# The first 32 places of experts 0 to 3 as a group of their own, ahead of the last choice

## The chip, the cores and the metric

The kernel runs on one core of a Trainium2 chip. The metric is the time of one execution on the device, in microseconds (us); the median of the runs counts.

## What is computed

The reference is a Fourier mixing layer followed by a mixture of experts with a capacity.

```python
X = np.fft.rfft(x, axis=1)                       # x: 8 x 2496 x 256
Yr = Xr @ w_r - Xi @ w_i + b_r                   # and Yi; then a soft threshold of 0.01 on both
y = np.fft.irfft(Yr + 1j * Yi, n=2496, axis=1)   # 19968 tokens of 256
expert_idx = np.argmax(y @ w_gate, axis=1)       # 8 experts
gate_w = softmax(y @ w_gate)[chosen expert]
for e in range(8):
    tok_idx = the 80 tokens of expert e with the largest gate_w
    h = np.maximum(y[tok_idx] @ w1[e], 0.0)      # w1: 256 x 1024
    out[tok_idx] = gate_w[tok_idx, None] * (h @ w2[e])   # w2: 1024 x 256
```

All other rows of the output are zero.

## The kernel before

The eight samples go one after another through stages of products (the transforms, the complex weights, the threshold), which `stageD` and others issue; that is some 490 us of the time. Per sample the gates of all tokens are computed, and the best candidates of every expert are kept. Of the mixed tokens only partial sums are stored to HBM, in two tensors `hd[0]` (7 rows of 256 f32 for each set of tokens) and `hd[1]` (6 rows): a token is a sum of these 13 rows with 13 weights out of the table `vt`.

**The choice.** The choice among the first samples is held as `bg`: a list `t0b` of 80 values for each of the 8 experts, sorted, and a list of their places (`t1b`, then `pfb`). The last samples give a list of 48 (`NEW`), and `merge` compares it from the end with the places 32 to 79 of the first list, and puts the better of the two there. The places 0 to 31 are those of the first samples whatever the last ones bring. A flag tells whether the two lists may have been too short, and then a slow branch at the end repeats the choice (here it isn't taken). `choose` spreads the 8 x 80 places over 640 partitions in 5 groups of 128: `flat` multiplies on VectorE (L1017) with an identity of 8, and TensorE sums over 8 partitions (L1021), and L1284 to L1286 make `posA`, the addresses. `rows` does the same for the gate values.

**The gathers.** For each of the 5 groups GpSimd issues, through `gather` (L1109), a gather of token numbers (`tok`), of 128 x 1792 values (`hx`, from `hd[0]`), of 13 weights (`wv`) and of 128 x 1536 values (`hx`, from `hd[1]`). `begin` writes them out for groups 0 to 2; those of groups 3 and 4 follow as buffers come free (3 buffers for the larger part, 2 for the smaller).

**The sums.** `position` makes the weighted sum of a group's 13 rows. For groups 0 and 1 some rows (`PEQ`) go to TensorE as products with a diagonal matrix of weights (`columnsY`, L1224, which also transposes), the others to ScalarE (L1162) and VectorE (L1170). For groups 2 to 4 ScalarE (L1185, L1190), VectorE (L1197, L1198) and GpSimd (L1193) share them, and TensorE transposes the sum (L1228). In both cases ScalarE writes the columns as f16 to `xT` (L1231) and VectorE the f16 rest (L1232): one eviction.

**The experts.** Expert e uses the columns 80e to 80e+79 of `xT`: `ffn1` (L1245, 96 products of 128x80, first layer, evicted by L1247 on ScalarE and L1249 on VectorE) and `ffn2` (L1261, 96 products, evicted into `oT` by L1262). Expert 3 ends with place 319 and needs groups 0 to 2, expert 4 also group 3. `give` transposes 128 rows of results (L1266), multiplies by the gate (L1268) and scatters them (L1269).

**The weights.** Each expert's weights are loaded as f32 in 4 pieces of 512 KB (L823), cast to f16 on ScalarE (L840, L843, L846; `prepW`) and the residue is taken on GpSimd (L858) or VectorE (L848). Those of experts 6 and 7 come last: two pieces of expert 6 are loaded from SyncE at 510.06 us, behind the last stores, and expert 7's go into buffers of the gathers once these are free. Fillers on TensorE (L1701, 6 of them, and `busy`, L1210, up to 36) stand before the first group's products.

**What sets the order.** Each engine executes its own list in order; the lists come from a scheduler that places an instruction where its inputs are ready by its own estimate, except where `tc.issue_after(i)` or `behind(event)` puts it after a named instruction.

## Time and profile before

| | us |
|---|---|
| median of 3 runs | 583.82 (583.77 to 584.67) |
| profiled execution, its time | 588.99 |
| profiled execution, its span | 587.2 |
| TensorE busy | 532.3 (91%) |
| VectorE busy | 388.1 (66%) |
| GpSimd busy | 376.7 (64%) |
| ScalarE busy | 324.6 (55%) |

A share of busy time is a mean over the whole span. The change concerns only the last 100 us or so, where the choice ends, the groups are gathered and the experts run; that stretch has to be read by its own rows, below. Times in the rows are counted from the start of the span.

### The profile page before, as it was taken

The page shows a single profiled execution, that of the slowest core. Times are in us where ns is not written, and L with a number is a line of the kernel's source. Part 1 is how long each engine was busy: PE and PEld are TensorE (multiplying, and loading weights), DVE is VectorE, ACT ScalarE, POOL GpSimd, SP SyncE. Part 2 cuts the span into 40 slices and gives each one's busy share as a digit, 9 for nine tenths or more (in the row PEclk, how much of TensorE's full clock was granted, in tenths as well). Part 3 has the DMA queues.
Part 4 walks back from the last instruction along what each step waited for, and adds up shares of the span by engine and source line. Part 5 has one row for each costly group of instructions (what it writes and reads, how often), then busy time and mean ns, then how long its engine had stood idle before and what let it go on. Part 6 is the DMA issues. An engine that isn't in the chain of part 4 may idle for free.

```text
span 587.2 us, 12890 instructions
## 1 busy us (share of the span) xinstructions
PE 532.3 (91%) x5037; PEld 387.2 (66%) x5037; DVE 388.1 (66%) x739; ACT 324.6 (55%) x466; POOL 376.7 (64%) x301
## 2 busy tenths in 40 slices
PE   7869999999999999999999999988899988885883
PEld 3356676668677866877687778756767865444883
DVE  4423555666767667667667876768999687844750
ACT  2324868575756756565667565555654447321671
POOL 4005887686857677786768775777961575765671
PEclk9969999999999999999999999998999868885998
DMA  7897898997989799978979787999936796677530
GB/s 220 256 244 210 308 216 275 265 283 217 282 267 312 193 259 269 278 217 238 280 250 258 235 255 181 304 263 270 230 114 193 185 316 202 176 251 259 189 96 23
DMA packets 97225, 137.02 MB, mean 233 GB/s; under 512 B 26601, under 2 KB 77809, under 8 KB 95403
## 3 DMA queue, kind: packets, MB, share of 16 engines
q1 hardware_dynamic: 91115, 118.10, 69.8%
q0 software_dynamic: 2624, 11.45, 5.8%
q10 hardware_dynamic: 3418, 6.58, 3.5%
q8 instruction: 41, 0.67, 0.5%
q14 instruction: 27, 0.21, 0.1%
HBM read 70.82 MB, written 65.29 MB: 232 GB/s over the span
## 4 chain that ended last, share of the span: by engine, by line
PE 43%; DVE 15%; DMA 13%; issue 10%; POOL 9%; ACT 6%; SPq 2%; POOLq 0%; ACTq 0%; DVEq 0%
PE ps L443 21%; PE ps L311 5%; DMA wt<-in_moe_w 4%; PE ps L609 4%; DMA xt<-in_x 2%; DVE R L472 2%; POOL R L475 2%; ACT tp L467 2%; PE ps L546 2%; DMA out<-zero 2%; PE ps L547 2%; PE ps L382 1%; PE ps L383 1%; PE ps L384 1%; PE pf L1245 1%
## 5 line engine op out<-in xcount | busy, mean ns | idle before, releaser
L443 PE MATMUL ps<-XT,WM 128*128 128x288 f16 (+4 forms) x1536 | 215.7, 297 | 7.5 <-DVE Gs L561 2.1
L443 PEld LDWEIGHTS <-WM 128*128 128x128 f16 x1536 | 148.7, 98 | 64.2 <-issue 7.5
L472 DVE SCALAR_TENSOR_TENSOR R<-ps,thr,tp 128x674 f32<-128x674 f32 (+1 forms) x56 | 48.6, 868 | 75.8 <-ACT tp L467 72.1
L490 POOL TENSOR_TENSOR YT<-R,YT 128x1408 f16<-128x1408 f32 (+1 forms) x28 | 73.4, 2623 | 32.0 <-ACT YT L489 30.2
L467 ACT ACTIVATE tp<-ps,thr 128x674 f32<-128x674 f32 (+1 forms) x56 | 43.5, 777 | 80.4 <-PE ps L443 80.4
L475 POOL TENSOR_TENSOR R<-R,sgs 128x576 f32<-128x576 f32 x28 | 36.5, 1302 | 75.0 <-DVE R L472 75.0
L297 POOL TENSOR_TENSOR xs<-xt,xs 117x1024 f16<-117x1024 f32 (+1 forms) x39 | 76.2, 1955 | 9.9 <-ACT xs L296 9.8
L382 PE MATMUL ps<-t2s,z 128*128 128x128 f16 x320 | 59.7, 225 | 10.3 <-DMA z<-zs 7.4
L388 DVE TENSOR_TENSOR XT<-ps,XT 128x640 f16<-128x640 f32 (+2 forms) x64 | 51.7, 815 | 18.4 <-ACT XT L387 17.7
L333 DVE TENSOR_TENSOR zs<-ps,zs 128x1024 f16<-128x1024 f32 (+1 forms) x45 | 51.1, 1136 | 18.1 <-ACT zs L332 17.7
L383 PE MATMUL ps<-t2s,z 128*128 128x128 f16 x320 | 59.7, 225 | 0.0
L384 PE MATMUL ps<-t2s,z 128*128 128x128 f16 x320 | 59.7, 225 | 0.0
L387 ACT ACTIVATE XT<-ps 128x640 f16<-128x640 f32 (+2 forms) x64 | 44.4, 700 | 25.6 <-PE ps L384 24.4
L311 PE MATMUL ps<-xs,t1s 117*128 117x512 f16 x213 | 52.6, 379 | 1.0 <-POOL xs L297 0.8
L609 PE MATMUL ps<-YO,vqs 128*128 128x512 f16 (+1 forms) x252 | 48.7, 334 | 1.1 <-DVE hs L616 1.1
L332 ACT ACTIVATE zs<-ps 128x1024 f16<-128x1024 f32 (+1 forms) x45 | 42.9, 954 | 12.0 <-PE ps L311 6.9
L558 DVE TENSOR_TENSOR YO<-ps,YO 128x768 f16<-128x768 f32 (+1 forms) x50 | 45.4, 907 | 6.2 <-ACT YO L557 6.2
L489 ACT ACTIVATE YT<-R 128x1408 f16<-128x1408 f32 (+1 forms) x28 | 35.5, 1267 | 21.3 <-POOL R L486 21.2
L546 PE MATMUL ps<-wgi,YT 128*128 128x144 f16 (+1 forms) x302 | 44.3, 232 | 2.8 <-DVE R L472 1.6
L547 PE MATMUL ps<-wgi,YT 128*128 128x136 f16 (+1 forms) x302 | 43.5, 228 | 0.0
L557 ACT ACTIVATE YO<-ps 128x768 f16<-128x768 f32 (+1 forms) x50 | 38.4, 774 | 3.1 <-PE ps L547 1.1
L609 PEld LDWEIGHTS <-vqs 128*128 128x128 f16 x252 | 24.6, 99 | 23.3 <-issue 2.9
(320 smaller groups left out, 990.5 us busy)
## 6 DMA issues: line engine op xcount, KB each, us to landing
out<-zero SPq DMA_DIRECT2D x48, 384.0 KB
hd<-hs SPq DMA_DIRECT2D x94, 192.0 KB
z<-zs SPq DMA_DIRECT2D x35, 512.0 KB
xt<-in_x SPq DMA_DIRECT2D x41, 312.0 KB
z<-z SPq DMA_DIRECT2D x14, 528.0 KB
z<-z SPq DMA_DIRECT2D x14, 432.0 KB
wt<-in_moe_w ACTq DMA_DIRECT2D x10, 512.0 KB
pair<-in_moe_w SPq DMA_DIRECT2D x10, 512.0 KB
```

Of the source, the lines that this page charges most:

```text
L297: nc.gpsimd.tensor_tensor(xs[:, 1, :ng], xt[:, j0:j0 + ng], xs[:, 0, :ng], op=ALU.subtract)
L311: nc.tensor.matmul(pt[:, 512 * j:512 * j + 512], t1s[:, t], xs[:, h, 2 * j:2 * j + 2], start=(i == 0), stop=(i == 2))
L382: nc.tensor.matmul(o, zz(0), t2s[:, cl, 0, :], start=True, stop=False)
L383: nc.tensor.matmul(o, zz(0), t2s[:, cl, 1, :], start=False, stop=False)
L384: nc.tensor.matmul(o, zz(1), t2s[:, cl, 0, :], start=False, stop=True)
L443: nc.tensor.matmul(pt[:, o:o + e - a], WM[:, dh, m, wh, 128 * eh:128 * eh + 128], XT[:, dh, xh, c, a:e], start=(i == 0), stop=(i == len(te ...
L467: acts.append(nc.scalar.activation(fv(t), pv, AF.Relu, bias=thr[:, eh, ri, 0:1]))
L472: nc.vector.scalar_tensor_tensor(fv(Rf), pv, thr[:, eh, ri, 1:2], fv(t), op0=ALU.add, op1=ALU.min)
L490: nc.gpsimd.tensor_tensor(yv(1), rv, yv(0), op=ALU.subtract)
L546: nc.tensor.matmul(pt[:, off:off + w], yt(0), wgi[:, eh, 0:w], start=True, stop=False)
L547: nc.tensor.matmul(pt[:, off:off + w - w % 128 // 2], yt(1), wgi[:, eh, 0:w - w % 128 // 2], start=False, stop=True)
L609: nc.tensor.matmul(o, tab[:, v], yo(h), start=(i == 0), stop=(i == 2))
```

## The change

The places 0 to 31 of experts 0 to 3 (128 places, since nothing that comes later can change them) become a group of their own, number 4 (`NL`). A new function `ahead_` works out their addresses as soon as the combination of the last samples' sums is done, and gathers their tokens, rows and weights, into memory (`pair6`) that expert 6's weights get later. `scaleA` multiplies the 13 rows by their weights on ScalarE, and `columnsA` adds and transposes them by 26 f32 products with the identity (52 records in a trace). The remaining 512 places are four groups: 48 of each of the experts 0 to 3, then 80 of each of the experts 4 to 7. Experts 0 to 3 need groups 0 and 1, expert 4 groups 1 and 2, experts 6 and 7 group 3.

With this go other changes: `BUSY` 32 to 12; the products of `flat` are cut by the parts of the list (192 and 320 columns, and 128); the columns of groups 0 and 1 are evicted in two pieces each, and the outputs of experts 0 to 3 also in two; the stores of the last stage are staged in one memory; the residues of expert 5's second layer go from GpSimd to VectorE; the casts of expert 6's weights, and their residues, go behind work of groups 2 and 3; two loads of expert 6's weights go behind the flag; expert 7's weights are loaded into the memory of expert 0's.

```diff
+SURE = CAP - NEW
+EARLY = ((0, 4, 0, SURE),)
+LATER_ = ((0, 4, SURE, CAP), (4, 8, 0, CAP))
...
-        hs = wkb.tile([128, 3, 256], F32, name="hs", bufs=3) if (ch, x) != (1, 2) else newYO(0).bitcast(F32).rearrange("p h j e -> p (h j e)")[:, :768].rearrange("p (c e) -> p c e", e=256)
+        if ch and x == 1:
+            hlast.append(newYO(0).bitcast(F32).rearrange("p h j e -> p (h j e)"))
+        hs = hlast[0][:, 768 * x:768 * x + 768].rearrange("p (c e) -> p c e", e=256) if ch else wkb.tile([128, 3, 256], F32, name="hs", bufs=3)
...
-    WV = [(6, 0, 0), (6, 0, 1)] + [(6, 1, 0), (6, 1, 1)] + [(7, 1, 1)]
+    WV = [(5, 1, 0), (5, 1, 1), (6, 0, 0), (6, 0, 1)] + [(6, 1, 0), (6, 1, 1)] + [(7, 1, 1)]
...
-                wt = p5.tile([128, 7 - i, 256], F32, name=f"hx{i}", bufs=3 - i).rearrange("p r e -> p (r e)")[:, :1024]
+                wt = slots["pair0"][:, 1024 * (2 * k + i):1024 * (2 * k + i) + 1024]
...
-                with behind(("A", "ra", 4)) if (e, k) == (7, 1) else tc.issue_after((hevs if e == 6 else dev)[-1].ins):
+                with behind(("A", "ra", k)) if e == 6 else tc.issue_after(dev[-1].ins):
...
-            nc.vector.tensor_tensor(px, v.unsqueeze(1).to_broadcast([8, 8, n]), i8.unsqueeze(2).to_broadcast([8, 8, n]), op=ALU.mult)
+            o = 0
+            for e0, e1, r0, r1 in parts:
+                k, w = e1 - e0, r1 - r0
+                nc.vector.tensor_tensor(px[:, o:o + k * w].rearrange("p (e r) -> p e r", e=k), v[:, r0:r1].unsqueeze(1).to_broadcast([8, k, w]), i8[:, e0:e1].unsqueeze(2).to_broadcast([8, k, w]), op=ALU.mult)
+                o += k * w
...
-    BUSY = (6, 32)
+    BUSY = (6, 12)
...
+        if e < 4:
+            nc.scalar.activation(oT[:, :, w * e:w * e + w], pv[:, :, SURE:], AF.Copy)
+            nc.scalar.activation(oT[:, :, 128 * NL + SURE * e:128 * NL + SURE * e + SURE], pv[:, :, :SURE], AF.Copy)
...
+    def ahead_():
+        p = spare()[:8]
+        pt = psum()
+        nc.vector.tensor_copy(pt[:8, 512:512 + SURE], bg[1][:, :SURE])
+        pr = flat(pt[:8, 512:512 + SURE], EARLY, F16, px=p.bitcast(F16))
+        nc.vector.tensor_tensor(posA[:, NL:], pr, cbs[:, 0, NL:], op=ALU.add)
+        hA = p7.tile([128, 4096], F32, name="pair6")
+        ct, get = gather_ids("A", posA, NG, cid[0:R1])
+        wv = hA[:, 3328:3344]
+        with tc.issue_after(sums[-1].ins):
+            get(NL)
+            gather(hA[:, :1792], hd[0][:5 * 192], ct[:, NL, 1:2])
+            gather(wv, vt, ct[:, NL, 2:3])
+            egs.append(gather(hA[:, 1792:3328], hd[1][:5 * 192], ct[:, NL, 1:2]))
+        return ct, [hA[:, 256 * r:256 * r + 256] for r in range(13)], wv
+
+    def scaleA(hx, wv):
+        for r in range(13):
+            nc.scalar.activation(hx[r], hx[r], AF.Copy, scale=wv[:, r:r + 1])
+
+    def columnsA(nm, hx):
+        pt = pct.tile([128, 512], F32, name="pt", bufs=1)
+        for h in range(2):
+            for r in range(13):
+                warms.append(nc.tensor.matmul(pt[:, 128 * h:128 * h + 128], hx[r][:, 128 * h:128 * h + 128], ident, start=(r == 0), stop=(r == 12)))
+        pv = pt[:, 0:256].rearrange("p (h e r) -> p h e r", h=2, e=4)
+        xv = lambda l: xT[:, l].rearrange("p h (e r) -> p h e r", e=E)[:, :, 0:4, :SURE]
+        ev[nm, "ya"] = nc.scalar.activation(xv(0), pv, AF.Copy)
+        nc.vector.tensor_tensor(xv(1), pv, xv(0), op=ALU.subtract)
...
-        got.append(gather_h(nm, 2, ct, True, lambda: get(4)))
+        got.append(gather_h(nm, 2, ct, True))
...
     combine(YO)
+    stacks[5].close()
+    p7 = ctx.enter_context(tc.tile_pool(name="p7", bufs=1, side="right", reuse_waits="tile"))
+    ctA, hxA, wvA = ahead_()
...
-        sA = begin("A", NG, posA, cid[0:R2])
+        with tc.issue_after(fls[-1].ins):
+            columnsA("A", hxA)
+        with tc.issue_after(warms[-1].ins):
+            busy(BUSY[1], pairs[0, 0][0])
+        sA = begin("A", NL, posA, cid[0:R2], ctA)
```

How this moves instructions is shown at three places.

GpSimd, from the combination's last addition to the first late gathers (`L858` before and `L867` now are residues of weights, `pair_6558` is the early group's memory), before:

```order
L574 TENSOR_TENSOR YO_6518<-YO_6518 128x768
L858 TENSOR_TENSOR pair_6789<-wt,pair_6789 128x1024 x2
L858 TENSOR_TENSOR pair_6789<-pair_6451,pair_6789 128x1024 x2
L1109 DMA tok<-cid,posA 128x4 x2
L1109 DMA hx_6754<-hd_104,tok 128x1792
L1109 DMA wv<-in_vt,tok 128x16
L1109 DMA hx_6758<-hd_105,tok 128x1536
```

and now:

```order
L581 TENSOR_TENSOR YO_6518<-YO_6518 128x768
L1124 DMA tok<-cid,posA 128x4
L867 TENSOR_TENSOR pair_6855<-wt,pair_6855 128x1024
L1124 DMA pair_6558<-hd_104,tok 128x1792
L1124 DMA pair_6558<-in_vt,tok 128x16
L1124 DMA pair_6558<-hd_105,tok 128x1536
L867 TENSOR_TENSOR pair_6855<-wt,pair_6855 128x1024
L1124 DMA tok<-cid,posA 128x4 x2
L1124 DMA hx_6821<-hd_104,tok 128x1792
L1124 DMA wv<-in_vt,tok 128x16
```

The early group's four gathers stand between the combination and the late groups' first token gather, with one residue between its token gather and its rows and one behind them; of the four residues two are left there.

SyncE's queue, from the last stores (`hd`) on: the loads of weights of experts 6 (`pair_6451`) and 7 (four of 512 KB), and the reading of the flag, before:

```order
L600 DMA hd_105<-YO_6666 64x768
L823 DMA pair_6451<-in_moe_w 128x4x256 x2
L1737 TENSOR_LOAD flag
L1737 ISA x2
L823 DMA hx_7585<-in_moe_w 128x1024
L823 DMA hx_7593<-in_moe_w 128x4x256
L823 DMA hx_7589<-in_moe_w 128x1024
L823 DMA hx_7597<-in_moe_w 128x4x256
```

and now:

```order
L607 DMA hd_105<-YO_6663 64x768
L1810 TENSOR_LOAD flag
L1810 ISA x2
L835 DMA pair_6451<-in_moe_w 128x4x256 x2
L835 DMA pair_5064<-in_moe_w 128x1024
L835 DMA pair_5064<-in_moe_w 128x4x256
L835 DMA pair_5064<-in_moe_w 128x1024
L835 DMA pair_5064<-in_moe_w 128x4x256
```

The two loads into `pair_6451` went from ahead of the flag to behind it, and expert 7's four now go to `pair_5064`, the memory of expert 0's weights, and not to `hx`.

ScalarE, from the outputs of expert 1 to the columns of the group that expert 4 waits for, before (group 2's columns are `L1231` of the first rows, group 3's that at the end):

```order
L1262 ACTIVATE wt<-pf 128x2x80
L1190 ACTIVATE hx_6863<-hx_6863,wv 128x256 x2
L1185 ACTIVATE yp<-hx_6859,wv 128x256
L1231 ACTIVATE xT<-pt 128x2x128
L1268 ACTIVATE og<-ps,gateA 128x256
L1247 ACTIVATE hp<-pf 128x320 x2
L840 ACTIVATE pair_6451<-hx_7585 128x1024
L1262 ACTIVATE wt<-pf 128x2x80
L1231 ACTIVATE xT<-pt 128x2x128
```

and now (`L855` and `L852` are casts of weights, `L1290` and `L1291` the two pieces of an expert's outputs; the `L1256` at the end is group 2's, which expert 4 now waits for):

```order
L1290 ACTIVATE wt<-pf 128x2x48
L1291 ACTIVATE wt<-pf 128x2x32
L1273 ACTIVATE hp<-pf 128x320
L1206 ACTIVATE hx_6889<-hx_6889,wv 128x256 x2
L1273 ACTIVATE hp<-pf 128x320
L852 ACTIVATE pair_6451<-pair_5064 128x1024 x2
L1201 ACTIVATE yp<-hx_6885,wv 128x256
L1290 ACTIVATE wt<-pf 128x2x48
L1291 ACTIVATE wt<-pf 128x2x32
L1256 ACTIVATE xT<-pt 128x2x128
L1299 ACTIVATE og<-ps,gateA 128x256
L1273 ACTIVATE hp<-pf 128x320 x2
```

The columns of one group fewer stand before expert 4; casts of experts 6's and 7's weights, which stood elsewhere or behind, stand between the groups.

## Rows read from the trace of the kernel before

**Rows 1.** Head of the page.

```profile
span 587.2 us, 12890 instructions
```

**Rows 2.** Chain of waits, 508 to 533 us: start, duration, what.

```profile
508.10 2.88 DMA hd<-hs
510.98 5.17 DMA tok<-cid,posA
...
519.70 6.69 DMA hx<-hd,tok
...
528.98 4.17 issue
```

**Rows 3.** Timeline of VectorE: start, us, line, operation, count, [idle before <- releaser].

```profile
508.26 0.20 DVE L1037 TENSOR_TENSOR Gs<-pfn,pfb 8x48 f32<-8x48 f32 x1
...
508.95 0.81 DVE L1017 TENSOR_TENSOR Gs<-pfb,eye 8x640 f16<-8x640 f32 x1
```

**Rows 4.** Timeline of GpSimd, 499 to 520 us.

```profile
499.17 4.21 POOL L858 TENSOR_TENSOR pair<-wt,pair 128x1024 bf16<-128x1024 f32 x2
...
510.98 1.06 POOL L1109 DMA_INDIRECT tok<-cid,posA  x1 [3.44 <-DMA hd<-hs]
...
518.45 0.95 POOL L1109 DMA_INDIRECT wv<-in_vt,tok  x1 [0.30 <-issue]
519.70 0.95 POOL L1109 DMA_INDIRECT hx<-hd,tok  x1 [0.30 <-issue]
```

**Rows 5.** Stretches: length, engines' busy time, granted clock, share of transfers, GB/s.

```profile
497.00:507.00 10.00, 10.00 (x31) 5.53 (x31) 9.48 (x38) 4.56 (x7) 9.92 (x6) 1.00 0.39 93
...
508.00:515.00 7.00, 4.94 (x24) 3.28 (x25) 3.87 (x22) 2.99 (x4) 2.02 (x2) 0.69 0.95 288
515.00:519.00 4.00, 4.00 (x14) 1.60 (x13) 2.33 (x2) 1.63 (x2) 1.72 (x2) 0.70 0.14 30
519.00:529.00 10.00, 7.99 (x44) 4.44 (x42) 4.30 (x11) 1.07 (x3) 7.56 (x9) 1.00 0.96 331
...
519.00:541.00 22.00, 12.74 (x95) 8.46 (x93) 9.22 (x22) 3.04 (x7) 14.72 (x15) 0.77 0.91 311
```

**Rows 6.** Timeline of SyncE's queue, weight loads.

```profile
510.06 1.16 SPq L823 DMA_DIRECT2D pair<-in_moe_w  x2
547.60 9.93 SPq L823 DMA_DIRECT2D hx<-in_moe_w  x3
```

**Rows 7.** Timeline of TensorE, 514 to 544 us.

```profile
514.81 8.99 PE L1210 MATMUL pf<-pair 128*128 128x512 f16 x35 [0.24 <-DVE ff L1056]
...
526.53 1.58 PE L1224 MATMUL ps<-wt,hx 128*128 128x128 f32 x12 [1.27 <-DMA hx<-hd,tok]
...
539.79 0.76 PE L1245 MATMUL pf<-xT,pair 128*128 128x80 f16 x9 [0.44 <-issue]
540.35 2.91 PE L1224 MATMUL ps<-v3s,hx 128*128 128x128 f32 x12
```

**Rows 8.** Timeline of TensorE, 553 to 571 us.

```profile
553.27 0.23 PE L1245 MATMUL pf<-xT,pair 128*128 128x80 f16 x2 [0.91 <-ACT xT L1231]
...
557.92 0.41 PE L1228 MATMUL pt<-ident,y 128*128 128x128 f32 x2 [1.05 <-DVE y L1198]
558.81 0.23 PE L1245 MATMUL pf<-xT,pair 128*128 128x80 f16 x2 [0.47 <-ACT xT L1231]
...
569.45 0.38 PE L1245 MATMUL pf<-xT,pair 128*128 128x80 f16 x6 [0.40 <-issue]
570.21 0.66 PE L1245 MATMUL pf<-xT,pair 128*128 128x80 f16 x14 [0.38 <-issue]
```

**Rows 9.** Timeline of ScalarE, 545 to 569 us.

```profile
545.44 1.70 ACT L1190 ACTIVATE hx<-hx,wv 128x256 f32<-128x256 f32 x4
...
558.37 0.38 ACT L1231 ACTIVATE xT<-pt 128x256 f16<-128x256 f32 x1 [0.36 <-PE pt L1228]
...
568.24 1.06 ACT L840 ACTIVATE pair<-hx 128x1024 f16<-128x1024 f32 x1 [0.81 <-DMA hx<-in_moe_w]
```

106 lines of the change are left out of this document (67 added, 39 removed).

## The prediction

> **What bounds the kernel now.** The profiled execution took 588.99 us, of which 587.2 is the span [rows 1]; the median of the runs is 583.82, that is 5.17 less. I make the sum as differences inside the profiled execution and put them on the median. A difference of 0.2% (1.17 us) is about what a measurement of this kernel can tell from no change.
>
> I read the chain of waits first, from the last choice to the end. Behind the choice stand transfers, not arithmetic [rows 2]: the gather of the first group's token numbers takes 5.17 us from its issue to what it releases, the gather of its rows 6.69, and before the first expert's products stand 4.17 us in which the trace shows no releaser. VectorE works without a pause on the last choice (the small steps on 8 partitions and the 640 columns wide product, [rows 3]), and GpSimd, done at 507.5 with four weight residues, of which two are shown, idles 3.44 us before the first gather [rows 4]. The table of stretches [rows 5] shows what the transfers do meanwhile: 288 GB/s in 508 to 515, nearly nothing (30) in 515 to 519, then 331 until 529 and 311 over the whole of 519 to 541. What fills 508 to 515 is the last stage's stores and two weight loads of 512 KB issued at 510.06 [rows 6].
>
> TensorE is not the limit there: 35 filler products, then the first group's products as its rows land [rows 7], then the first expert's, with six gaps of 0.17 to 1.21, together 3.10 us, without a releaser, the last of them before 539.79 [rows 7], when the transfers run dry. From 544 on the TensorE timeline [rows 8] shows short waits, always at a group's columns: 0.91, 1.05 and 0.47 around groups 2 and 3, then two gaps of 0.40 and 0.38 in expert 6's and 7's products, where the last weights come late. So two stages: until 541 transfers bound, after it ScalarE and VectorE, which make the columns of groups 2, 3 and 4, against TensorE.
>
> **The change, part by part.**
>
> *The choice on VectorE.* Three operations come between the last choice's steps: a cast of 8x32, a product of 8x128 and an addition of 128x1. An 8x48 step is 0.20, the 8x640 product 0.81 [rows 3], so 8x128 comes to 0.20 + 80/592 x 0.61 = 0.28. The cast and the product lie on the path: 0.4. The addition fits the half microsecond in which VectorE waits for TensorE there: 0. The late product is cut into 192 and 320 columns: 128 fewer (0.13) against one more start (0.14): 0.
>
> *GpSimd.* After the combine's last addition (the residues begin behind it at 499.17) now stand the early token gather, one of the four residues (4.21 for two, [rows 4]), three gathers, a second residue, and then the first late gather. The other two residues (expert 5's second layer) go to VectorE, into the place of two residues of the same size that leave there for later: nothing. Early token gather 499.5 to 500.5, residue to 502.7; if its landing also takes 5.17, the row gathers start at 505.5, and with 1.25 from one to the next [rows 4] they end at 509.0, the residue at 511.4, the late token gather begins at 511.65 instead of 510.98. If the landing takes only 2.9 (the store in [rows 2]), GpSimd waits for the choice instead. Together with the choice +0.4 to +0.7; I take +0.6, since all of GpSimd's 3.44 of cover is used up.
>
> *The two weight loads.* They move from 510.06 to behind the flag and the residues on VectorE, about 517.5. The token gather then no longer shares 508 to 515 with 1.05 MB: a gain between 0 and 2.3 (5.17 down to the store's 2.88). In exchange the 1.05 MB meet the first group's rows: at 311 GB/s (the mean of 519 to 541) that is 3.4 us, of which between 0 and 3.4 falls on those rows. I take 1.2 on both sides, so 0 net, nearer the low end, because the hole of 515 to 519 takes a part of the load.
> In total, the late groups gather 0.92 MB less before 541 and the loads add 1.05 MB: 0.13 MB more, 0.4 us.
>
> *TensorE before the first group.* 52 records of 128x128 f32 products and 12 fillers replace 32 fillers. A record took 1.58/12 = 0.13 at the full clock and 2.91/12 = 0.24 at half [rows 7]. The clock stands at half until about 517.4 (mean 0.70 over 515 to 519, [rows 5]): 11 records by then, 41 more by 522.8, 12 fillers of 0.22 (the 35 took 8.99, 2.6 of it at half: 7.7/35) by 525.4. The twelve products of the first group that follow wait for rows until 526.53, so this costs nothing, if the clock rises. ScalarE's 13 scalings (0.40 each, as the four in [rows 9]) run ahead of it in time in which it waited for gathers.
>
> *Evictions.* The early columns and the pieces into which groups 0 and 1 are now written add two small ScalarE and two VectorE operations to each group's path: +0.4 on group 0, +0.2 on group 1.
>
> *How much of this arrives.* 0.6 + 0.4 + 0.4 = 1.4 us later at the first expert's first product. But its end (540.55) is set by gaps that last as long as the transfers; 3.1 us of gaps, and the 4.17 without releaser ahead of them [rows 2], are there to take it. I take the end of that expert's first layer as unchanged, between -1.0 and +2.0.
>
> *The rest.* Experts 0 to 3 now bring 48 late places each, not 80: 128 rows fewer, so expert 4 waits for group 2, not group 3. Between the evictions of groups 1 and 2 ScalarE has 12 scalings and starts, 6 output evictions and 5 activations, at most 0.40 each, and 4 weight casts of 1.06 [rows 9]: at most 13.4 us, and 12.2 with the evictions, which are less than half as wide, at half. It came out of group 1's eviction at 544.6 (two operations ahead of the 545.44), now 0.2 later: 557.0 to 558.2 for group 2's eviction. Before, group 3's stood at 558.37. I take 557.8, since its activations also wait for products: -0.6. Behind it one group fewer goes through TensorE (0.41 [rows 8]), and expert 7's weights, which now go to the memory of expert 0's weights as soon as those are used instead of into the gather buffers from 547.60 on [rows 6], come before they are needed: the 0.40 and 0.38 go. The one group more that is scattered at expert 4 adds nothing to the end; the last scatter is as before. Sum: -0.6 - 0.41 - 0.78 = -1.8, so 582.0.
>
> **The rivals.**
>
> *R1, full gain.* ScalarE keeps ahead, and TensorE alone sets the rest: 0.91 + 1.05 + 0.47 go as well: -2.43 - 1.19 = -3.6, 580.2; with 1.0 from an earlier token gather, 579.2. For it: the low end of ScalarE's sum leaves 1.4 us. Against it: 12 us of ScalarE stand between groups 1 and 2, with four casts that were not there before.
>
> *R2, slower: the moved weight loads.* The whole 3.4 us falls on the first group's rows and nothing absorbs it: 0.6 + 2.2 (3.4 less 1.2) + 0.4 + 0.3 (the transfers' end) = 3.5 later, less 1.8: +1.7, 585.5. It decides where the first expert's first layer ends later than about 542.4. For it: from 519 to 529 the transfers are at 0.96 of their time [rows 5], with no room. Against it: the hole of 515 to 519, and the gaps that may swallow it.
> The Trainium skill ("DMA: Bandwidth & Descriptors", section "Queues, rings and completion order") says that a DMA engine goes round its queues packet by packet; by that rule loads and gathers would each get half while both last, so that the whole 1.05 MB comes out of the gathers' time, and the time would be R2's. The trace has no stretch in which the rows of a gather and a weight load stand side by side, so it neither agrees nor differs.
>
> *R3, the clock.* The identity products do not raise TensorE's clock as the f16 fillers did, and it stays at half: 52 x 0.24 = 12.5, then 12 fillers of 0.44, so 532.6 instead of 526.5, +6.1 - 1.8 = +4.3, 588.1. Against it: in 497 to 507 TensorE did f32 products only, without a pause, at a granted clock of 1.00, and kept 1.00 through 519 to 529, f32 products in its last part [rows 5].
> The Trainium skill ("TensorE: Matmul & The Clock Gate", Part 4) says that products with the identity in transpose mode do not engage the full clock; by that the time would be R3's. These are plain products, and no row here shows the clock rise on f32 products alone, only hold.
>
> *R4, nothing moved.* Group 4's work lay beside other work anyway, and the four casts take its place on ScalarE: 583.8. Against it: the 0.40 and 0.38 and the 0.41 of a group's columns are on TensorE itself.
>
> **How the numbers follow.** The forecast 582.0 has 0.47, with its own range 580.9 to 583.3 (0.2 for a fifth of it above 582.65, the bound of faster); R1 0.2, R2 0.2, R3 0.08, R4 0.05. Faster: 0.2 + 0.8 x 0.47 = 0.57. Same (582.65 to 584.99): 0.09 + 0.05 + the low part of R2 0.04 = 0.18. Slower: 0.25. The range goes from R1 with an early token gather (579.2) to just past R2 (585.9); R3 and a little at each end stay out.
>
> **What would show it.** Right: late token gather at 511.2 to 511.7, landing in under 5; the first expert's first layer ends within 1 us of 540.55; group 2's columns at 557 to 558; no gaps in experts 6 and 7. Wrong: granted clock 0.50 through the identity products (R3); rows of group 0 landing after 529 (R2); TensorE without waits from 545 on (R1); group 2's columns after 559, behind ScalarE's casts (R4).

## The result, and the profile after

The changed kernel takes **576.69 us** (574.14 to 578.89, 4 runs) against 583.80 for the kernel before, measured beside it: a ratio of 0.9878, with 0.9829 to 0.9926 as its interval, or 7.1 us less. The prediction was 582.0, with a range of 579.2 to 585.9: the direction was right, and the time lies below the range.

The profiled execution of the changed kernel took 574.14, the lowest of its four runs, and that of the kernel before 588.99, some 5 above its median; so the two traces differ by 14.85, twice what the times do, and 3.75 of that arises before the stretch that the change concerns. To compare traces I count from one event that the change leaves alone, the end of the combination's last addition on GpSimd (**E0**; 499.20 before, from 497.39 + 1.81, and 495.45 after, from 493.64 + 1.81). In the profiles of this study E0 lies anywhere from 494.93 to 500.96, whichever kernel it is.

The head of the page and the stretches of the changed kernel's profile (length, engines' busy time, granted clock, share of transfers, GB/s), as [rows 1, 5]:

```profile
span 572.4 us, 12944 instructions
```

```profile
515.00:519.00 4.00, 4.00 (x31) 3.05 (x30) 0.00 (x0) 0.00 (x0) 2.89 (x4) 1.00 1.05 403
519.00:541.00 22.00, 18.15 (x309) 16.12 (x308) 18.90 (x41) 13.00 (x32) 13.91 (x15) 0.92 1.02 378
511.25:515.25 4.00, 4.00 (x37) 3.96 (x37) 2.77 (x6) 0.67 (x2) 2.23 (x2) 1.00 0.28 36
515.25:537.25 22.00, 19.27 (x267) 16.42 (x266) 15.21 (x37) 9.77 (x24) 14.35 (x16) 0.92 1.03 386
```

The first two are the stretches of [rows 5] by the clock of the trace, the last two the same by E0, which lies 3.75 earlier here. By E0, TensorE is busy for 19.27 of the 22 us where it was for 12.74, and the transfers move 386 GB/s where they moved 311. The nearly empty stretch (30 GB/s before) is still there, at 36 GB/s; the 403 of 515 to 519 are what follows it.

GpSimd's timeline and VectorE's, at the choice, as [rows 4, 3]:

```profile
502.50 2.15 POOL L867 TENSOR_TENSOR pair<-wt,pair 128x1024 bf16<-128x1024 f32 x1
507.95 0.96 POOL L1124 DMA_INDIRECT tok<-cid,posA  x1 [3.31 <-DVE th L1060]
...
512.52 1.28 POOL L1124 DMA_INDIRECT hx<-hd,tok  x1 [2.37 <-ACT pair L1338]
```

```profile
502.71 2.00 DVE L1049 TENSOR_TENSOR Gs<-gh,t0b 8x48 f32<-8x48 f32 x1
```

GpSimd still waits 3.31 for the choice. Its late token gather is issued 12.50 behind E0, against 11.78 before, and releases the first late rows after 4.57 (512.52 - 507.95), against 5.99.

TensorE's timeline from the identity products to the second group's products, and then its rows with waits until the end, as [rows 7, 8]:

```profile
511.36 6.07 PE L1344 MATMUL pt<-ident,pair 128*128 128x128 f32 x52
517.27 2.75 PE L1226 MATMUL pf<-pair 128*128 128x512 f16 x12
...
522.63 1.57 PE L1240 MATMUL ps<-wt,hx 128*128 128x128 f32 x12 [0.81 <-DVE xT L1348]
...
526.24 0.23 PE L1271 MATMUL pf<-xT,pair 128*128 128x80 f16 x2 [1.15 <-ACT xT L1256]
526.81 2.61 PE L1271 MATMUL pf<-xT,pair 128*128 128x80 f16 x46 [0.34 <-DVE xT L1258]
529.23 2.41 PE L1240 MATMUL ps<-v3s,hx 128*128 128x128 f32 x12
...
540.63 1.43 PE L1271 MATMUL pf<-xT,pair 128*128 128x80 f16 x35 [1.12 <-issue]
...
545.27 0.44 PE L1297 MATMUL ps<-ident,wt 128*128 128x128 f32 x2 [1.00 <-ACT wt L1290]
...
563.22 0.44 PE L1297 MATMUL ps<-ident,wt 128*128 128x128 f32 x2 [0.39 <-ACT wt L1293]
```

The first expert's first layer has no gaps inside (46 products in 2.61), and ends about where the second group's products begin, at 529.23. Behind it two waits of a microsecond and one of 0.39 stand; 0.91, 1.05, 0.47, 0.40 and 0.38 of [rows 8] are gone.

The table holds, for all kernels of the study, the median time, the ratio to the kernel before, measured beside it, with its interval, and from the trace, in us: **tok** and **rows**, the issue of the late token gather and of the first late rows, counted from E0; **L1**, the start of the second group's products, which mark the end of the first expert's first layer, counted from E0; **tail**, from there to the end of TensorE's last product; **end**, from E0 to the end of the span. Each of the last five columns is from one execution. The ratio of a_late leaves out one of its four executions, a slower one at a lower clock, which its median has.

| kernel | median | ratio | tok | rows | L1 | tail | end |
|---|---|---|---|---|---|---|---|
| before | 583.80 | 1 | 11.78 | 17.77 | 41.15 | 37.69 | 88.00 |
| b_again | 586.74 | 1.0008 (0.9981 to 1.0036) | 11.77 | 18.24 | 37.94 | 39.63 | 86.93 |
| b_again2 | 583.02 | 1.0002 (0.9969 to 1.0034) | 11.78 | 18.35 | 32.96 | 41.71 | 83.97 |
| b_loads | 582.48 | 0.9950 (0.9916 to 0.9985) | 10.94 | 14.67 | 36.27 | 39.25 | 84.37 |
| b_busy12 | 579.70 | 0.9942 (0.9913 to 0.9971) | 11.78 | 18.43 | 32.45 | 39.01 | 80.60 |
| b_loads_e7 | 578.22 | 0.9929 (0.9899 to 0.9959) | 10.94 | 14.35 | 32.92 | 37.69 | 79.44 |
| b_loads_e7b | 579.33 | 0.9934 (0.9902 to 0.9967) | 10.24 | 13.81 | 30.82 | 38.34 | 77.88 |
| b_all | 578.36 | 0.9917 (0.9883 to 0.9950) | 10.10 | 13.79 | 31.32 | 37.52 | 77.55 |
| after | 576.69 | 0.9878 (0.9829 to 0.9926) | 12.50 | 17.07 | 33.78 | 34.43 | 76.95 |
| a_again | 574.50 | 0.9861 (0.9837 to 0.9885) | 12.49 | 16.70 | 32.93 | 34.05 | 75.77 |
| a_ref | 574.99 | 0.9877 (0.9841 to 0.9914) | 12.49 | 16.89 | 33.54 | 34.00 | 76.41 |
| a_res | 577.98 | 0.9916 (0.9887 to 0.9945) | 16.65 | 19.90 | 34.14 | 35.30 | 78.42 |
| a_e7hx | 578.51 | 0.9921 (0.9895 to 0.9946) | 12.52 | 16.78 | 33.77 | 36.62 | 79.40 |
| a_late | 584.10 | 0.9877 (0.9781 to 0.9972) | 10.68 | 17.03 | 42.66 | 34.24 | 85.66 |
| a_late2 | 580.06 | 0.9954 (0.9934 to 0.9975) | 10.68 | 17.03 | 37.70 | 33.21 | 79.57 |
| a_busy32 | 580.20 | 0.9871 (0.9813 to 0.9929) | 12.51 | 16.81 | 37.96 | 34.74 | 81.60 |
| a_busy32b | 580.25 | 0.9959 (0.9937 to 0.9981) | 12.49 | 16.94 | 33.48 | 41.14 | 83.35 |
| a_b32ord | 576.44 | 0.9893 (0.9845 to 0.9941) | 12.50 | 16.88 | 34.44 | 34.20 | 77.51 |
| a_port | 576.77 | 0.9883 (0.9840 to 0.9926) | 10.66 | 17.92 | 33.29 | 34.09 | 76.04 |
| a_port2 | 576.14 | 0.9887 (0.9846 to 0.9928) | 10.70 | 16.93 | 32.20 | 33.66 | 74.47 |

### The profile page after: what moved, and what is told of

It reads as the page before. It is cut to its first block, busy times and chain, and to the rows that moved or that the text cites. A ratio compares the mean times of both kernels' runs of the same rounds, so it can differ in the third digit from the quotient of the medians.

```text
span 572.4 us, 12944 instructions
## 1 busy us (share of the span) xinstructions
PE 525.7 (92%) x5067; PEld 383.6 (67%) x5067; DVE 386.5 (68%) x741; ACT 328.1 (57%) x479; POOL 371.0 (65%) x295
## 5 line engine op out<-in xcount | busy, mean ns | idle before, releaser
L386 PE MATMUL ps<-t2s,z 128*128 128x128 f16 x320 | 57.8, 222 | 9.0 <-DMA z<-zs 7.2
L387 PE MATMUL ps<-t2s,z 128*128 128x128 f16 x320 | 57.8, 222 | 0.0
L388 PE MATMUL ps<-t2s,z 128*128 128x128 f16 x320 | 57.8, 221 | 0.0
L553 PE MATMUL ps<-wgi,YT 128*128 128x144 f16 (+1 forms) x302 | 43.2, 228 | 3.3 <-DVE R L479 1.9
```

The costliest lines, as they stand in the source:

```text
L386: nc.tensor.matmul(o, zz(0), t2s[:, cl, 0, :], start=True, stop=False)
L387: nc.tensor.matmul(o, zz(0), t2s[:, cl, 1, :], start=False, stop=False)
L388: nc.tensor.matmul(o, zz(1), t2s[:, cl, 0, :], start=False, stop=True)
```

## The experiments

**The two kernels again.** No edit. The kernel before:

> The kernel before, unchanged, for a second profile of it. Theories: A (ahead): the gain comes from one group's rows, tokens and weights being gathered before 508 instead of in the crowded stretch of 515 to 541. B (loads): it comes from the two weight loads leaving the stretch in which the first token numbers are gathered. C (clock and stalls): it comes from TensorE not standing before the first expert, so that its clock stays up. D (the profile): the first profile of before (588.99) was taken in an execution 5 us longer than its median, so that up to 5 of the 14.9 us between the two profiled executions are not the change. D expects here an execution of 583 to 585 with a span of 581 to 583, the choice's addresses 2 to 4 us earlier than 510.53, and the wait of 4.17 and the gaps of 3.10 in the first expert at half or less; A, B and C expect wait, gaps and half clock of the first expert as in the first profile.

> The kernel before, a third profile. If the pause belongs to the kernel: 6 us or more from the group's twelve products to the first layer, and 38 us or more from the combination's end to the second group's products. If it belongs to the execution: some 4 and some 35. The comparison in the choice 1.8 to 2.0 in either case, and the time within 1 us of the kernel before.

The changed kernel:

> The changed kernel once more, unedited, as the measure for the three kernels beside it. All theories expect 7 us less than the kernel before on the same chip (ratio 0.988), and a tail of about 34.4 us from the end of the first expert's first layer to the last product, against 37.7 to 39.6 in the kernel before.

> The changed kernel, unedited, a third time, as the measure for the three beside it: ratio 0.986 to 0.988 to the kernel before; the choice's first comparison on VectorE (8x48) takes 2.00 again, as long as GpSimd's residue beside it, and not the 0.20 of its neighbours.

The changed kernel repeats: L1 at 33 to 34, a tail of 34.0 to 34.4, and 7.9 and 7.3 us less than the kernel before beside it. The kernel before doesn't repeat inside: L1 lies at 41.15, 37.94 and 32.96, and where it is early the tail is long. The pause ahead of the first layer, 4.17 in [rows 2], comes again in b_again and in b_loads (below), here TensorE of each:

```profile
532.52 0.29 PE L1245 MATMUL pf<-xT,pair 128*128 128x80 f16 x2 [5.97 <-ACT xT L1231]
```

```profile
528.38 0.29 PE L1245 MATMUL pf<-xT,pair 128*128 128x80 f16 x2 [4.48 <-issue]
```

So of three profiles of the kernel before two have it, against what the expectation D had said of b_again; of the 17 other profiles of the study only that of b_loads has one over 1.71. In b_again2 it is 1.10, and two other waits stand there instead:

```profile
528.76 0.23 PE L1245 MATMUL pf<-xT,pair 128*128 128x80 f16 x2 [1.10 <-ACT xT L1231]
...
543.51 0.44 PE L1228 MATMUL pt<-ident,y 128*128 128x128 f32 x2 [2.48 <-DVE y L1198]
...
547.91 0.29 PE L1245 MATMUL pf<-xT,pair 128*128 128x80 f16 x2 [3.62 <-ACT xT L1231]
```

What the 3.62 waits for is seen on ScalarE and GpSimd of the same run. On ScalarE the two scalings of group 3's second rows stand ahead of group 2's columns (this is the order shown with the change, above), and wait 3.95:

```profile
546.28 0.91 ACT L1190 ACTIVATE hx<-hx,wv 128x256 f32<-128x256 f32 x2 [3.95 <-issue]
...
547.50 0.36 ACT L1231 ACTIVATE xT<-pt 128x256 f16<-128x256 f32 x1
```

```profile
535.21 0.94 POOL L1109 DMA_INDIRECT hx<-hd,tok  x1 [0.30 <-ACT hx L1190]
...
537.71 0.94 POOL L1109 DMA_INDIRECT hx<-hd,tok  x1 [0.30 <-PE pf L1245]
```

By GpSimd's order the gather at 535.21 is group 4's first rows and that at 537.71 group 3's second: the rows that are wanted first are issued behind the others, and the scalings that need them start 8.6 behind their issue. The profile names no releaser for the 3.95; that it is these rows follows from the order.

**The residues of expert 5, and with them the loads.** In the kernel before, the two residues go to VectorE, and both loads of expert 6's weights then follow the flag:

```diff
-    WV = [(6, 0, 0), (6, 0, 1)] + [(6, 1, 0), (6, 1, 1)] + [(7, 1, 1)]
+    WV = [(5, 1, 0), (5, 1, 1), (6, 0, 0), (6, 0, 1)] + [(6, 1, 0), (6, 1, 1)] + [(7, 1, 1)]
```

> The kernel before, with one part of the change: the residues of expert 5's second layer on VectorE instead of GpSimd, which holds back the two loads of expert 6's weights until after the flag. B: gives most of the gain, 4 to 7 us faster than before (577 to 580), token numbers landing in under 4 us instead of 5.17. A: between 1 us slower and 1.5 faster.

The opposite edit, in the changed kernel:

```diff
-    WV = [(5, 1, 0), (5, 1, 1), (6, 0, 0), (6, 0, 1)] + [(6, 1, 0), (6, 1, 1)] + [(7, 1, 1)]
+    WV = [(6, 0, 0), (6, 0, 1)] + [(6, 1, 0), (6, 1, 1)] + [(7, 1, 1)]
```

> The changed kernel with the two residues of expert 5's second layer back on GpSimd, and with them the two weight loads of expert 6 back ahead of the flag. Theory B (residues and loads carry part of the gain, as the 2.9 us of the same edit made in the kernel before): 2 to 3 us slower than the changed kernel, with the late addresses' token gather taking over 5.5 us to land again. Theory A (the early group alone carries it, and what the loads cost is hidden behind its products): within 0.7 us of the changed kernel. A third case: over 4 us slower, since GpSimd now has five gathers and four residues ahead of the late token gather (2.1 us each for the two residues, later by up to 4.2).

b_loads is 0.5% faster than the kernel before (2.9 us), and a_res 3.5 us slower than a_again beside it. I had costed the move of the residues at nothing. One reason is in the choice's 8x48 comparison on VectorE, which reads two operands in SBUF. VectorE and GpSimd of the kernel before, then of a_res:

```profile
505.86 1.75 DVE L1036 TENSOR_TENSOR Gs<-gh,t0b 8x48 f32<-8x48 f32 x1
```

```profile
503.34 4.21 POOL L858 TENSOR_TENSOR pair<-pair,pair 128x1024 bf16<-128x1024 f32 x2
```

```profile
505.64 6.15 DVE L1049 TENSOR_TENSOR Gs<-gh,t0b 8x48 f32<-8x48 f32 x1
```

```profile
505.44 2.13 POOL L867 TENSOR_TENSOR pair<-wt,pair 128x1024 bf16<-128x1024 f32 x1
507.52 4.20 POOL L867 TENSOR_TENSOR pair<-pair,pair 128x1024 bf16<-128x1024 f32 x2
```

The comparison ends at 507.61 and 511.79, where GpSimd's residues end (507.55 and 511.72): it stands still while they run. In b_loads, where they have ended, it takes 0.20, and the late addresses come 0.84 sooner; there the token gather also lands in 3.73 (510.80 - 507.07) and not 5.99, with the loads behind it. So of the 3.1 by which the first late rows come sooner (14.67 against 17.77) the addresses bring 0.84, and the landing 2.26, which goes with the loads. The two were not run apart. VectorE and GpSimd of b_loads:

```profile
503.50 0.20 DVE L1036 TENSOR_TENSOR Gs<-gh,t0b 8x48 f32<-8x48 f32 x1
```

```profile
507.07 1.06 POOL L1109 DMA_INDIRECT tok<-cid,posA  x1 [6.77 <-DVE th L1047]
...
510.80 0.94 POOL L1109 DMA_INDIRECT hx<-hd,tok  x1 [1.41 <-DMA tok<-cid,posA]
```

The Trainium skill ("SBUF — State Buffer", section "Who interferes with whom") says that a VectorE instruction with two SBUF inputs and a GpSimd instruction that reads SBUF exclude one another, the later waiting for the earlier; the trace agrees, with 0.20 alone and 1.75 to 6.15 beside residues (a_res goes further than that, see the last section). The prediction called GpSimd's 3.44 of idle time cover; its own residues had made part of it.

**Is there more to gain there?** One residue still stands beside the comparison in the changed kernel (2.00). a_port puts it ahead of the early rows' gathers, a_port2 onto VectorE:

```diff
-                    with tc.issue_after((egs if (e, k, i) > (5, 0, 0) else sums)[-1].ins) if sums and e > 4 else ExitStack():
+                    with tc.issue_after((egs if (e, k, i) > (5, 0, 1) else sums)[-1].ins) if sums and e > 4 else ExitStack():
```

```diff
-    WV = [(5, 1, 0), (5, 1, 1), (6, 0, 0), (6, 0, 1)] + [(6, 1, 0), (6, 1, 1)] + [(7, 1, 1)]
+    WV = [(5, 0, 1), (5, 1, 0), (5, 1, 1), (6, 0, 0), (6, 0, 1)] + [(6, 1, 0), (6, 1, 1)] + [(7, 1, 1)]
```

> The changed kernel with its second residue on GpSimd moved from behind the early group's last gather to behind the first residue, so that no residue runs while VectorE makes the choice's 8x48 comparison; the early rows are gathered 2.1 us later for it. Theory P (a VectorE step that reads two operands from SBUF stands still for as long as GpSimd's residues last): the comparison takes 0.20, the late addresses come 1.8 us sooner after the combination's end, and the kernel is 1 to 1.8 us faster than the changed one. Rival (the early rows matter more than the addresses): the same time or slower, with the identity products waiting for rows.

> The changed kernel with that second residue on VectorE, behind the flag, instead of on GpSimd: neither the comparison nor the early rows are held. Theory P: comparison 0.20, late addresses 1.8 us sooner, 1.0 to 1.8 us faster than the changed kernel, if the 1.2 us more on VectorE stand in its wait for the first late rows. Rival: those 1.2 us push the diagonals of weights for the first late group's products, and half of the gain or all of it is lost.

The comparison takes 0.20 in both, and the late token gather is issued 1.8 sooner; yet the times (576.77, 576.14) are not below a_ref's 574.99 beside them, so the expected gain of 1 to 1.8 is not seen (the intervals, some 2.4 us to either side, could hide one of 1). It goes at once into the token gather's landing. GpSimd of a_port:

```profile
511.62 0.94 POOL L1124 DMA_INDIRECT tok<-cid,posA  x1 [1.55 <-DVE th L1060]
...
518.88 0.94 POOL L1124 DMA_INDIRECT hx<-hd,tok  x1 [5.06 <-ACT pair L1338]
```

7.26 from one to the other, against 4.57: the late rows are issued 17.92 and 16.93 behind E0, and in the changed kernel 16.70 to 17.07. The early group's rows, gathered from 506.58 on, are still being moved: a scaling on ScalarE that waits for them starts at 517.17. The stretch of a_port in which the landing falls, and that scaling:

```profile
512.00:519.00 7.00, 6.04 (x33) 5.19 (x33) 3.52 (x10) 4.73 (x12) 1.63 (x3) 0.76 0.91 324
```

```profile
517.17 2.50 ACT L1338 ACTIVATE pair<-pair 128x256 f32<-128x256 f32 x6 [0.55 <-DMA pair<-hd,tok]
```

In a_port2, which gathers the early rows as early as the changed kernel, the landing takes 6.23 all the same (516.96 - 510.73). By the trace's packets the last stage's stores are moved until about 515 there, and until about 511 in the changed kernel, and the tokens' own few KB only at their end. So an earlier address gains nothing while early rows and stores are on their way. The scalings on ScalarE, which the profile names as releaser of the first late rows, cannot all be what these wait for: in a_port they end at 519.67, behind the issue at 518.88.

Where no early rows are gathered and these residues and the loads are moved (b_loads, b_loads_e7, b_loads_e7b, b_all), the late rows come at 13.8 to 14.7.

**Expert 7's weights.** In the changed kernel back into the gathers' buffers:

```diff
-                wt = slots["pair0"][:, 1024 * (2 * k + i):1024 * (2 * k + i) + 1024]
+                wt = p5.tile([128, 7 - i, 256], F32, name=f"hx{i}", bufs=3 - i).rearrange("p r e -> p (r e)")[:, :1024]
```

> The changed kernel with expert 7's weights back in the gather buffers, as before, so that they come as those buffers get free. Theory E (this memory is what takes the last two waits away and keeps TensorE the bound of the tail): 0.8 us slower (0.40 and 0.38 back), up to 2 if group 3's columns come later too. Theory A (the group alone): no difference over 0.5 us, because with four late groups the buffers get free earlier than with five.

and in b_loads the opposite edit:

> The kernel before, with the residues of expert 5's second layer on VectorE (and so the loads behind the flag) and with expert 7's weights in the memory of expert 0's, but without the early group. If these two parts add up: 2.9 and 0.8, so 3.7 us less than the kernel before (ratio 0.9937), and the other half of the gain is the group's. If the early group is only a part of no consequence: 7 us less. If expert 7's memory is worth nothing without the group, since the columns of group 4 come last anyway: 2.9 less, 0.995.

> The kernel before with residues on VectorE, loads behind the flag and expert 7's weights in expert 0's memory, once more. If the parts are what took the pause away: again 33 us from the combination's end to the second group's products; if the execution: 33 to 37. Time 3.5 to 4.5 less than the kernel before.

a_e7hx is 4.0 us slower than a_again beside it, the tail 2.6 longer: more than either theory said. The last cast of expert 7's weights waits on ScalarE, and an output eviction with it, for which TensorE waits. ScalarE and TensorE of a_e7hx:

```profile
554.54 1.06 ACT L852 ACTIVATE pair<-hx 128x1024 f16<-128x1024 f32 x1 [1.84 <-SPq L1811]
555.50 0.29 ACT L1293 ACTIVATE wt<-pf 128x160 f32<-128x160 f32 x1
```

```profile
555.84 0.44 PE L1297 MATMUL ps<-ident,wt 128*128 128x128 f32 x2 [1.90 <-ACT wt L1293]
```

These waits are some 2 of the 4.0. b_loads_e7 is 4.2 and 4.0 us below the kernel before, in line with the 3.7 expected of residues, loads and memory; the interval of b_loads is too wide to give the memory's share by itself. L1 of b_loads_e7b (30.82) is earlier than either expectation, and the pause is in neither of the two.

**The place of the early gathers.** In the changed kernel, the three row and weight gathers of the early group go behind the first two late token gathers, and the scalings and identity products behind those:

```diff
-            get(NL)
-            gather(hA[:, :1792], hd[0][:5 * 192], ct[:, NL, 1:2])
-            gather(wv, vt, ct[:, NL, 2:3])
-            egs.append(gather(hA[:, 1792:3328], hd[1][:5 * 192], ct[:, NL, 1:2]))
+            egs.append(get(NL))
+        def three():
+            gather(hA[:, :1792], hd[0][:5 * 192], ct[:, NL, 1:2], True)
+            gather(wv, vt, ct[:, NL, 2:3], True)
+            gather(hA[:, 1792:3328], hd[1][:5 * 192], ct[:, NL, 1:2], True)
+        fours.append(three)
...
         get(1)
+        if fours:
+            fours.pop()()
```

> The changed kernel, with the early group's rows and weights gathered only behind the first two late token gathers (its token gather stays early); its scalings and identity products follow then. A: loses most of the gain, 4 to 7 us slower than the change (581 to 584), because 1.71 MB come back into the crowded stretch (4.4 us at 390 GB/s) and three more issues (3.75 us) stand before the first group's rows. B and C: within 2 us of the change (576 to 579), since loads and fillers stand as in the change.

> The changed kernel with the first group's gathers behind the late token gathers once more, since its first timing (ratio 0.978 to 0.997) told nothing. Theory A (that the group is gathered ahead is worth something): 3 to 6 us slower than the changed kernel. Rival N (only the numbers matter: four late groups, expert 7's memory, the residues; the place of the early gathers doesn't): within 1 us of it, because the late addresses come 1.8 us sooner and the first expert can wait for the bytes either way.

The first timing (584.1, ratio 0.9781 to 0.9972, 4 runs) was too wide to tell anything. The second gives 580.06, 5.1 us above a_ref beside it, as theory A said: that the group goes ahead is worth 5 in this kernel, L1 being 4 later. TensorE of a_late2 shows where: it idles until the early rows are scaled, and the identity products stand ahead of the first late group's.

```profile
520.64 8.44 PE L1348 MATMUL pt<-ident,pair 128*128 128x128 f32 x52 [7.90 <-ACT pair L1342]
```

**The number of fillers.** `BUSY = (6, 32)` to `(6, 12)` in the kernel before, and the opposite in the changed one, nothing else:

> The kernel before with 12 fillers behind the flag instead of 32, and nothing else. If the fillers make no difference (they stand in a wait for rows): within 1 us of the kernel before. If they keep the clock up that the first group's products need: 2 to 4 us slower, with a clock of 0.50 at those products. If the many fillers are what holds the products up: 2 to 3 faster.

> The changed kernel with 32 fillers before the first group's products again instead of 12. C as a matter of too many fillers: 20 more of 0.22 push the first group's products from 522.6 to 524.4 or so, 1.5 to 2.5 us slower than the change. A and B: the products wait for rows anyhow, 0 to 1.8 slower.

> The changed kernel with 32 fillers, as before, instead of 12, once more, since its profile showed a first layer that ended 38 us behind the combination's end and its times did not. If the fillers hold up the first late products: 26 fillers more by 0.22 come to some 4 us later, partly covered by the wait for rows, and 1 to 3 us slower than the changed kernel (ratio 0.990). If not: 0.986 to 0.988.

I had costed this at nothing. b_busy12 is 3.4 to 3.6 us faster than the kernel before. The changed kernel with 32 fillers took 580.20 and 580.25; its first ratio, of 4 runs, tells it from nothing, by the second (10 runs) it is 4.7 to 5.7 slower than with 12 (0.9959 against 0.9861 to 0.9878), more than the 1 to 3 expected. The fillers' own time is one part of it. In a_busy32 the clock stood at 0.51 over 515 to 521, the 52 identity products took 8.79, the fillers 7.07 behind them without a pause, and the first late products came after both, so that L1 is 4 later:

```profile
515.00:521.00 6.00, 6.00 (x31) 5.95 (x32) 2.77 (x6) 0.93 (x3) 4.48 (x4) 0.51 0.54 164
```

In a_busy32b they took 6.07 and 7.07, and L1 lies at 33.48, as early as with 12; there the loss is in the tail, and this is the other part: the number enters the scheduler's estimate, and GpSimd's order comes out differently. With 12 fillers and then with 32 (`hx_6839` is `hx_6859` under another number, both group 2's second rows, and `hx_6885`, `hx_6905` group 3's first):

```
L1124 DMA wv<-in_vt,tok 128x16
L1124 DMA hx_6839<-hd_105,tok 128x1536
L1124 DMA hx_6885<-hd_104,tok 128x1792
L1124 DMA wv<-in_vt,tok 128x16
...
L1124 DMA wv<-in_vt,tok 128x16 x2
L1124 DMA hx_6905<-hd_104,tok 128x1792
L1124 DMA hx_6859<-hd_105,tok 128x1536
```

GpSimd, ScalarE and TensorE of a_busy32b show what this does:

```profile
530.14 1.03 POOL L1124 DMA_INDIRECT wv<-in_vt,tok  x1 [2.62 <-ACT hp L1273]
531.47 0.94 POOL L1124 DMA_INDIRECT hx<-hd,tok  x1 [0.30 <-DVE y L1186]
532.72 1.62 POOL L1124 DMA_INDIRECT hx<-hd,tok  x1 [0.31 <-DMA hx<-hd,tok]
```

```profile
543.06 0.91 ACT L1206 ACTIVATE hx<-hx,wv 128x256 f32<-128x256 f32 x2 [7.67 <-DMA hx<-hd,tok]
```

```profile
544.26 3.36 PE L1287 MATMUL pf<-hp,pair 128*128 128x80 f16 x48 [6.67 <-ACT wt L1291]
```

Group 2's second rows are issued at 532.72, behind a weight gather of group 3 that waited 2.62; in the changed kernel at 526.23; that is 35.9 behind E0 against 30.8. ScalarE waits for them for 7.67, with the outputs of an expert in line behind, and TensorE for 6.67. In b_busy12 the like pair is turned the other way than in b_again2 above: group 3's second rows are issued ahead of group 4's first; whether its 3.4 come from that order or from the fillers' time no run tells.

To tell order from time, a_b32ord keeps 32 fillers and chains group 3's gathers behind group 2's, which gives GpSimd the order of the changed kernel:

```diff
-    BUSY = (6, 12)
+    BUSY = (6, 32)
...
-                S["got"].append(gather_h(S["nm"], g + 3, S["ct"]))
+                S["got"].append(gather_h(S["nm"], g + 3, S["ct"], S["nm"] == "A"))
```

> The changed kernel with 32 fillers, and with the gathers of group 3 chained behind those of group 2 on GpSimd, which is the order that they have with 12 fillers. Theory O (the order): as fast as the changed kernel, ratio 0.986 to 0.988, no stretch of 3 us with under 0.3 MB moved between 520 and 540, and no wait of ScalarE over 2 us for rows of group 2. Rival F (the time of the fillers): as slow as with 32 fillers alone, 0.993 to 0.996.

576.44, a tail of 34.20, and ScalarE's wait is 0.69:

```profile
542.97 0.91 ACT L1206 ACTIVATE hx<-hx,wv 128x256 f32<-128x256 f32 x2 [0.69 <-DMA hx<-hd,tok]
```

So it is, in that execution, the order for the larger part: 3.8 of the 4.7 to 5.7 are back, by ratios whose intervals just touch (0.9845 to 0.9941 and 0.9937 to 0.9981), and the wait and the tail show where they were lost. The ratio, 0.9893, lies between those of the two theories, nearer to O's; the sign of 0.3 MB tells nothing, since a_busy32b has no such stretch either (the least of 3 us, counted from 520 on, is 163 GB/s, some 0.5 MB).

**What the group itself is worth.** b_all is the kernel before with the three parts that were found to matter and need no group: the edits of b_loads_e7 and 12 fillers. What else the change brings (the moved casts of expert 6's weights, the eviction in pieces, the staging of the last stores, and the last stage's products put in a fixed order, which the change also does) is not in it, and stays in what is called the group's here.

> The kernel before with all that needs no early group: the residues of expert 5's second layer on VectorE, expert 7's weights in expert 0's memory, 12 fillers. Theory A (the group is worth 3 us or more beside them): 578 to 579, 4 to 5 less than the kernel before, and waits for the columns of groups 2 and 3 in the tail, of 1.0 and 0.5 each. Theory N (the group is worth nothing beside them): 575 to 576, as the changed kernel.

578.36, 4.0 below the kernel before (4.8 by the ratio), as theory A said; b_loads_e7 and 3.4 for the fillers don't add, since 4.2 was there without them. The changed kernel is 2.3 to 3.3 below b_all by the ratios (0.9917 against 0.9878, 0.9861 and 0.9877). The intervals overlap for all three, and none of these was measured beside b_all; taken together they give some 2.9, with 2.2 to either side (an estimate, from the four intervals). So a gain of the group is likely, and its size is not settled. By the table, with one trace of b_all, the group costs 2 in L1 (31.32 against 33 to 34) and gains 3.3 in the tail (37.52 against 34.2). b_all's waits in the tail are those that I had read in [rows 8]. TensorE of b_all:

```profile
544.87 0.41 PE L1228 MATMUL pt<-ident,y 128*128 128x128 f32 x2 [1.54 <-DVE y L1198]
545.76 0.23 PE L1245 MATMUL pf<-xT,pair 128*128 128x80 f16 x2 [0.47 <-ACT xT L1231]
...
555.09 0.23 PE L1245 MATMUL pf<-xT,pair 128*128 128x80 f16 x2 [0.47 <-ACT xT L1231]
```

## Why the prediction was wrong

*The choice and GpSimd, +0.6.* Right in size: 12.50 against 11.78 behind E0, +0.72. It came by the second way that the prediction names: the early tokens land soon (the row gathers start 3.38 behind the token gather), and GpSimd waits for the choice, 3.31. What it had not read is that VectorE stands 2.00 there for GpSimd's residue, as it did before for 1.75. Without the move of the two residues the term would have been +4.9 (a_res, 16.65). "Nothing" for that move was a mis-sized term: 2.9 to 3.5, together with the loads.

*The loads, 0 net.* The landing lost 1.4 of 5.99, inside the bound of 2.3. The rows took 10.1 to 10.7 to the twelve products, against 9.56, 7.74 and 8.82 in the three profiles of the kernel before: 0.6 to 3 more, inside the bound of 3.4. That the empty stretch would take a part of the load was wrong (36 GB/s in it). R2 did not come: L1 lies far below the 43.2 behind E0 (542.4) that it asked for.

*The identity products, 0.* Right: 52 records in 6.07, done with their 12 fillers 2.6 before the twelve products. R3 did not come (below). The 32 fillers taken to 12 were wrong at 0, in the changed kernel for the order more than for their time.

*"The rest", -1.8.* **This term failed, in the stage that I had put at -0.6.** The tail is 34.16 on the mean of three profiles of the changed kernel against 39.68, so -5.5, and against the one profile of before that I read (37.69) still -3.3 to -3.7. I had three parts in it. From the columns that expert 4 waits for to the end I forecast -1.19; it is 18.43 to 18.45 in the changed kernel against 19.67, 19.73 and 18.45, so -0.8 on the mean: right. From L1 to group 1's columns nothing changes, as assumed (3.4 and 3.3 on the mean). In between, from group 1's columns to those that expert 4 waits for, I forecast 14.00 to become some 13.2 (the -0.6 and the 0.2 that group 1 was to be later); it is 12.12, 12.59 and 12.54, against 14.00, 16.02 and 21.09, so -4.6 on the mean. This stretch in the changed kernel, in the profile that I read, and in b_again2 (ScalarE's busy time is the fifth number):

```profile
533.09:545.21 12.12, 10.01 (x264) 9.51 (x261) 9.77 (x22) 11.37 (x29) 8.12 (x9) 1.00 0.68 254
```

```profile
544.37:558.37 14.00, 11.72 (x293) 11.13 (x291) 10.40 (x26) 9.72 (x25) 8.56 (x12) 0.99 0.65 200
```

```profile
533.16:554.25 21.09, 13.21 (x293) 12.33 (x290) 12.47 (x28) 9.83 (x26) 12.64 (x15) 0.84 0.74 253
```

So ScalarE's sum does bind in the changed kernel, as I had said (11.37 of 12.12, and one of the two waits of a microsecond on TensorE is for ScalarE's outputs); the sum of 12.2 to 13.4 was only a little large. What I had wrong is the kernel before: there ScalarE has 9.72, 9.81 and 9.83 of work in 14.00, 16.02 and 21.09, and waits for the rest, as in b_again2 for rows that GpSimd issues behind others wanted later. I had counted from the 14.00 of one profile, the shortest of three. R1, to which I gave 0.2 and 3.6, is right from 545.66 on, where TensorE has no wait until the last 0.39, and not before. Group 2's columns stand at 545.21, 49.8 behind E0, against 58.6 in the forecast: 1.1 of that is this stretch, all else that group 1's columns come sooner.

*"I take the end of that expert's first layer as unchanged".* **For the profile that it was read from, this step failed too**, and by more: L1 is 33.78, 32.93 and 33.54 in the changed kernel against 41.15 there. I took the pause of 4.17 and the gaps of 3.1 for a property of the stage, set by the transfers. In the other two profiles of the kernel before L1 is 37.94 and 32.96; on the mean it is 3.9 earlier now, against b_again2, whose execution (583.77) lies nearest to the medians of the kernel before, 0 to 0.8 later. So L1's part of the gain differs between executions: the pause stands in two of the three and in b_loads, and in none of the changed kernel. What makes it stays open: ScalarE's first columns wait there (532.72 in [rows 2]'s profile) with no releaser that the profile shows.

3.9 and 5.5 are more than 7.1 to 7.9; the profiled executions of the kernel before and after differ by more than the medians do, and no run tells why. Against b_again2 alone it is 0 to -0.8 and 7.3 to 7.7. The range was built on one profile of the kernel before, and could not hold waits that this profile does not show.

The parts don't add up. Taking back the residues with the loads, expert 7's memory, the place of the gathers or the number of fillers costs 3.5, 4.0, 5.1 and some 5, and all of it together is 7 to 8. For expert 7's memory and the fillers the rows above show a wait that comes back and that the other parts do not cover; for the whole sum this is argued, not shown. a_port, and a_port2 with the shortest end of all profiles (74.47), are not faster than the changed kernel by their times, so no version beats it.

## What to carry to other kernels

An engine that runs its list in order passes on every late input to all that stands behind it: before a stage is priced, its gathers and evictions have to be read in the order of their issue, and a number that only pads the program can turn that order. A pause without a releaser, and the length of a stage, are worth a second and a third profile of the same kernel before they are taken as room or as work. And idle time of GpSimd ahead of a step of VectorE is no cover if GpSimd's own work is what holds VectorE up.

## What was unexpected of the hardware

VectorE's comparison waited not for one instruction of GpSimd but for all three that followed one another: 6.15 beside residues of 2.13 and 4.20 (the second row is two), with no turn between them, though two of the three began after it. The search's steps beside the residues (MAX8 and its kin, 8x256) kept their 0.40.

TensorE's clock rose on f32 products with the identity alone. In a_late2 nothing else ran on it from 520.64 on, for 8.44, after an idle stretch. The stretches of a_late2 (the column before the share of transfers is the granted clock, 0.50 being 1.2 GHz and 1.00 2.4):

```profile
520.00:523.00 3.00, 2.36 (x11) 2.37 (x12) 0.00 (x0) 2.90 (x7) 2.09 (x4) 0.50 1.04 408
523.00:526.00 3.00, 3.00 (x17) 2.80 (x17) 0.39 (x2) 2.87 (x7) 2.39 (x3) 0.70 1.01 398
526.00:529.00 3.00, 3.00 (x29) 2.99 (x28) 2.35 (x6) 0.52 (x2) 0.96 (x2) 1.00 1.02 408
```

What R3 draws on in the Trainium skill ("TensorE: Matmul & The Clock Gate", Part 4) speaks of products in transpose mode; these are plain ones, so the trace neither bears it out nor speaks against it. How soon the clock rises differs between executions: in a_busy32 it stood at 0.51 over 515 to 521 while the same 52 products ran, for 8.79 instead of 6.07.
